# Value-weight loads issued from ScalarE, and a new order of the first value products, in a layernorm, memory-attention and gated-MLP kernel

## The chip, the cores and the metric

The kernel runs on one core of one Trainium2 chip. The metric is the device time of one execution in microseconds (us). The kernel before has a median of 689.46 us in three runs (689.43 to 689.73). Engines are named as the profile names them: PE is TensorE's matmuls, PEld its weight loads, DVE is VectorE, ACT is ScalarE, POOL is GpSimd and SP is SyncE. Loads and stores are DMAs that an engine issues; SPq, ACTq and POOLq are the issuing queues of those engines.

## The reference

One input `x` of 2048 tokens by 448 features goes through a layernorm; attention with a compressed memory over four segments of 512 tokens, and a gated MLP, both read the normalised rows, and their outputs are added to `x`:

```python
x = A_x                                   # 1 x 2048 x 448
xn = _layernorm(x, axis=-1)
return x + _A_ref(xn, A_wq, A_wk, A_wv, A_wo, A_beta) + _B_ref(xn, B_w_gate, B_w_up, B_w_down)
# _A_ref: 16 heads of 28; per segment a causal softmax attention, mixed by sigmoid(beta)
#         with a read of the memory M, z; then M += phi(k)^T v, z += sum phi(k)
# _B_ref: (sigmoid(xn @ w_gate) * (xn @ w_up)) @ w_down
```

What the change touches is the start: the layernorm of the first 512 tokens and `v = xn @ wv` for them.

## The kernel before, in words

The 2048 tokens are four blocks of 512 (`b`), each block four tiles of 128 tokens (`t`). A front part makes values, keys and queries for every block; from then on attention and the MLP are interleaved by a planner. Only the front of block 0 is touched, which is written out by hand: inside it the order of the instructions on PE, ACT and DVE is the order of the code, and the same holds for SP's queue.

Float32 products are made from two rounded parts. A matrix is copied into a rounded type (the high part), and the rest is a subtraction (the low part). A product is then high times high, high times low and low times high. The 448 features are three chunks of 128 and a tail of 64; the tail holds its high part in the upper half and its low part in the lower half of one chunk. So one product of a 128-token tile with the value weights is a list of 11 matmuls of 128 by 448. `EARLY[0]` (L52) lists them in the order that tile 0 and tile 1 use: terms 0 to 2 are high times high, terms 3 to 5 take the low part of the tokens, term 6 is the tail, terms 7 to 9 take the low part of the weights and term 10 the low part of the tail's weights. `value_terms(b, t, pv, terms, n0, n1)` (L333) issues terms n0 to n1.

For one tile the front does this:

- `statistics` (L294 to L296, DVE): mean and variance; `vh` is what the root reads.
- `root` (L301, ACT): a square root, `y`.
- `normalised` calls `rstd` (L308 to L311, DVE) and `normalise` (L320, DVE), which writes `xn`; a strip of 64 columns of it is copied on ACT (L324).
- `turn_high` (L95, PE): four transposes of `xn` into `pt`; then ACT copies the high part into `xs` (L97).
- `turn_low` (L102 and L103, DVE): the low parts of `xs`.
- `split_v(t)` (L431 on ACT, L432 on POOL): high and low part of chunk `t` of the value weights. `raw[0]` and `raw[1]` come from the first load of the weights, `raw[2]` and `raw[3]` from the second.
- `store_values` (L339, ACT): the finished product goes from PSUM to SBUF.

The loads of block 0 are issued by SP one after the other: token tile 0 (L409), tile 1 (L410), the value weights in two halves of 448 KB (L411, L412), token tiles 2 and 3 together (L413), and then the weights of keys and queries (L415 and on) and block 1 (L421). PE starts with 10 matmuls on an identity (`warm`, L442) that compute nothing that is used, and `fill(n)` (L445) issues n more of them; the profile counts two instructions for each.

After the four tiles, `values` for tile 3 and then `keys_queries` (L355, tile `pp`) for block 0 follow on PE.

Of the kernel before, what the change touches and what calls it, by code (L numbers as in the profile page):

```python
# [17 lines left out]
D = 448  # L18
# [33 lines left out]
EARLY = [HIGH + LOW_X + [(3, 3)] + LOW_W + [(3, 7)], HIGH + LOW_W + LOW_X + [(3, 3), (3, 7)]]  # L52
# [9 lines left out]
def kernel(  # L62
# [10 lines left out]
    nc = tc.nc  # L73
# [17 lines left out]
    def transpose_high(pt, src, dst, t):  # L91

        tok = slice(t * P, (t + 1) * P)
        for c in range(4):
            T.transpose(pt[:, c * P:(c + 1) * P], src[:, c * P:(c + 1) * P], ident)  # L95
        p3 = pt.rearrange("p (c n) -> p c n", c=4)
        A.activation(dst[:, 0:4, tok], p3, AF.Copy)  # L97
        return p3

    def transpose_low(p3, dst, t):  # L100
        tok = slice(t * P, (t + 1) * P)
        V.tensor_sub(dst[:, 4:7, tok], p3[:, 0:3], dst[:, 0:3, tok].bitcast(F32))  # L102
        V.tensor_sub(dst[64:, 3, tok], p3[64:, 3], dst[64:, 3, tok].bitcast(F32))  # L103
# [11 lines left out]
    def bank(name, tag):  # L115
        return ps.tile([P, L], F32, name=name, tag=tag, bufs=banks[tag])
# [32 lines left out]
    def four_k(dtype, name):  # L149
        return mid.tile([P, 2, L], dtype, name=name, tag="4k", bufs=4)  # L150
# [125 lines left out]
    with tc.tile_pool(name="front", bufs=2) as sb, tc.manual_schedule(engines=FRONT):  # L276
# [11 lines left out]
        def statistics(b, t0, steps):  # L288

            stats = sb.tile([P, steps, 6], F32, name=f"stats{steps}")  # L290
            mv = sb.tile([P, steps, 2], F32, name=f"mv{steps}")
            vh = sb.tile([P, steps], F32, name=f"vh{steps}")
            for t in range(steps):
                V.bn_stats(stats[:, t, :], acc[b][:, t0 + t, :])  # L294
                V.bn_aggr(mv[:, t, :], stats[:, t, :])
            V.tensor_scalar(vh, mv[:, :, 1], EPS, -0.5, op0=ALU.add, op1=ALU.mult)  # L296
            return mv, vh

        def root(vh):
            y = sb.tile([P, vh.shape[1]], F32, name=f"y{vh.shape[1]}")  # L300
            A.activation(y, vh, AF.Sqrt, scale=-2.0)  # L301
            return y

        def rstd(mv, vh, y):

            steps = vh.shape[1]
            tm = sb.tile([P, steps], F32, name=f"tm{steps}")
            V.reciprocal(y, y)  # L308
            if steps == 1:
                V.tensor_scalar(tm, y, y, vh, op0=ALU.mult, op1=ALU.mult)  # L310
                V.tensor_scalar(y, tm, 1.5, y, op0=ALU.add, op1=ALU.mult)  # L311
            else:
                V.tensor_mul(tm, y, y)
                V.tensor_mul(tm, tm, vh)
                V.scalar_tensor_tensor(y, tm, 1.5, y, op0=ALU.add, op1=ALU.mult)
            return [(mv[:, t, 0:1], y[:, t:t + 1]) for t in range(steps)]

        def normalise(b, t, mean, y):
            xn = sb.tile([P, 512], F32, name="xn")
            V.tensor_scalar(xn[:, :D].rearrange("p (m h c) -> p h m c", h=H, c=4),  # L320
                              acc[b][:, t, :].rearrange("p (h m c) -> p h m c", h=H, c=4), mean, y,
                              op0=ALU.subtract, op1=ALU.mult)
            if b == 0:
                A.activation(xn[:, D:], xn[:, 384:D], AF.Copy)  # L324
            else:
                G.tensor_copy(xn[:, D:], xn[:, 384:D])
            return xn
# [4 lines left out]
        def value_terms(b, t, pv, terms, n0=0, n1=len(TERMS)):  # L332
            for n in range(n0, n1):  # L333
                a, w = terms[n]
                T.matmul(pv[:, :D], xs[b][:, a, t * P:(t + 1) * P], wv[w],  # L335
                         start=n == 0, stop=n == len(TERMS) - 1)

        def store_values(b, t, pv):
            A.activation(vst[:, t, :, :DH], pv[:, :D].rearrange("p (h d) -> p h d", d=DH), AF.Copy)  # L339
            if t == NT - 1:  # L340
                nc.sync.dma_start(vd[b], vst.rearrange("p t h d -> p t (h d)"))
# [65 lines left out]
        raw = [four_k(F32, "wv_raw") for _ in range(2)]  # L407
        raw = [r.rearrange("p a n -> p (a n)")[:, :2 * D] for r in raw]
        nc.sync.dma_start(acc[0][:, 0, :], x[0:P, :])  # L409
        nc.sync.dma_start(acc[0][:, 1, :], x[P:2 * P, :])  # L410
        nc.sync.dma_start(raw[0], w_v[:, :2 * D])  # L411
        nc.sync.dma_start(raw[1], w_v[:, 2 * D:])  # L412
        nc.sync.dma_start(acc[0][:, 2:4, :], x[2 * P:L, :].rearrange("(t p) d -> p t d", p=P))  # L413
        raw = [raw[t // 2][:, t % 2 * D:(t % 2 + 1) * D] for t in range(4)]
        nc.sync.dma_start(stage[:, 0:2, :], w_qk[0:2].rearrange("c p n -> p c n"))  # L415
# [14 lines left out]
        def split_v(t):  # L430
            A.activation(wv[t], raw[t], AF.Copy)  # L431
            G.tensor_sub(wv[4 + t], raw[t], wv[t].bitcast(F32))  # L432
# [10 lines left out]
        def fill(n):  # L443
            for _ in range(n):
                T.matmul(warm[:, :P], ident, ident, start=True, stop=True)  # L445

        def turn_high(t):
            p3[t] = transpose_high(bank("pt", "s"), xn[t], xs[0], t)

        def turn_low(t):  # L450
            transpose_low(p3[t], xs[0], t)

        def normalised(t):
            xn[t] = normalise(0, t, *rstd(*st[t], y[t])[0])

        p3, xn, st, y = {}, {}, {}, {}
        st[0] = statistics(0, 0, 1)
        y[0] = root(st[0][1])
        normalised(0)
        st[1] = statistics(0, 1, 1)  # L460
        y[1] = root(st[1][1])
        turn_high(0)
        fill(5)
        split_v(0)
        split_v(1)
        normalised(1)
        split_v(2)
        split_v(3)
        turn_low(0)
        turn_high(1)  # L470
        st[2] = statistics(0, 2, 1)
        y[2] = root(st[2][1])
        turn_low(1)
        normalised(2)
        st[3] = statistics(0, 3, 1)
        pv = [bank("pv", "p") for _ in range(2)]
        for t in range(2):
            value_terms(0, t, pv[t], EARLY[0], 0, 7)
        value_terms(0, 0, pv[0], EARLY[0], 7)
        store_values(0, 0, pv[0])  # L480
        y[3] = root(st[3][1])
        turn_high(2)
        value_terms(0, 1, pv[1], EARLY[0], 7)
        store_values(0, 1, pv[1])
# [3 lines left out]
        pv = bank("pv", "p")  # L488
# [345 lines left out]
```

## Time and profile before

| | |
|---|---|
| median of three runs | 689.46 us (689.43 to 689.73) |
| the profiled execution's own time | 689.46 us |
| its span, first to last instruction | 687.7 us |
| PE busy in the span | 681.7 us (99%) |
| DVE, ACT and POOL busy | 567.4, 342.6 and 151.3 us |
| mean granted TensorE clock | 0.999 |

The span is 1.76 us shorter than the execution's own time; this rest lies around the instructions. A row of the timeline gives the start in us from the span's start, the duration in us, the engine, the line of the kernel, the operation, what it writes and reads, the shapes, how many instructions are merged in the row, and in brackets how long the engine was idle before and what released it. The line of DMA landings counts from the issue to the arrival.

### The profile page before, as it was taken

Reading aid. Unit: us, or ns where it says so; the run is one execution under the profiler, and the core shown is the slowest. Engines: PE = TensorE matmul, PEld = TensorE weight load, DVE = VectorE, ACT = ScalarE, POOL = GpSimd, SP = SyncE. Lnnn points to the kernel's source line nnn. Section 1 sums busy time; section 2 is a strip of 40 time slices with the busy share of each in tenths; the row PEclk is TensorE's granted clock in tenths of the full one; section 3 lists DMA queues with packets and bytes.
Section 4 is the critical chain, followed back from the end, with each engine's and each line's share of the span. In section 5 each row is a group of like instructions: output and inputs, shape, how many; then the busy total and the mean of one; then the engine's idle time right before and its main releaser. Section 6 shows DMA issues by size and latency. Waiting matters only on the chain.

```text
span 687.7 us, 10438 instructions
## 1 busy us (share of the span) xinstructions
PE 681.7 (99%) x3594; PEld 566.6 (82%) x3594; DVE 567.4 (83%) x994; ACT 342.6 (50%) x563; POOL 151.3 (22%) x349
## 2 busy tenths in 40 slices
PE   8999999999999999999999999999999999999997
PEld 7898888778878787787878878787787878878897
DVE  6765795767788988998898989989898899889863
ACT  4837555343554555543655446454653565446320
POOL 3500020101223222232332222322322322222000
PEclk9999999999999999999999999999999999999999
DMA  7446556696233323243223252314333332423342
GB/s 267 181 150 238 198 214 242 249 330 174 71 94 92 80 86 86 56 128 112 56 64 107 57 141 56 109 47 116 82 94 77 96 71 64 95 79 95 95 153 106
DMA packets 45796, 84.37 MB, mean 123 GB/s; under 512 B 6320, under 2 KB 20400, under 8 KB 45232
## 3 DMA queue, kind: packets, MB, share of 16 engines
q1 hardware_dynamic: 42736, 76.37, 35.8%
q0 software_dynamic: 3008, 7.34, 4.9%
q8 instruction: 28, 0.46, 0.3%
q14 instruction: 24, 0.20, 0.1%
HBM read 51.05 MB, written 32.64 MB: 122 GB/s over the span
## 4 chain that ended last, share of the span: by engine, by line
PE 70%; DVE 14%; issue 9%; POOL 4%; DMA 1%; ACT 1%; SPq 0%; POOLq 0%; ACTq 0%
PE pgu L247 26%; PE pd L173 13%; PE pp L355 10%; PE po L771 5%; PE pv L335 5%; PE st L612 3%; PE pa L687 3%; DVE mx L629 3%; DVE w L666 2%; POOL w L627 2%; DVE acc L174 2%; PE pmm L383 2%; PE n L401 2%; DVE hh L259 1%; DVE mx L633 1%
## 5 line engine op out<-in xcount | busy, mean ns | idle before, releaser
L247 PE MATMUL pgu<-xs,wgu 128*128 128x512 f32 x1232 | 304.1, 394 | 0.0
L247 PEld LDWEIGHTS pgu<-xs,wgu 128*128 128x128 f32 x1232 | 228.2, 188 | 47.4 <-issue 2.2
L173 PE MATMUL pd<-wdn,hh 128*128 128x448 f32 x672 | 156.0, 367 | 0.0
L627 POOL TENSOR_SCALAR_AFFINE_SELECT w<-w 128x256 f32<-128x256 f32 (+1 forms) x160 | 81.2, 509 | 236.4 <-ACT w L616 183.6
L173 PEld LDWEIGHTS pd<-wdn,hh 128*128 128x128 f32 x672 | 122.5, 188 | 12.3 <-issue 0.6
L667 ACT ACTIVATE w<-w 128x1024 f32<-128x1024 f32 (+1 forms) x96 | 87.3, 915 | 65.0 <-DVE w L666 64.2
L666 DVE TENSOR_TENSOR w<-w,mb 128x1024 f32<-128x1024 f32 (+1 forms) x96 | 98.9, 1045 | 0.1
L616 ACT ACTIVATE w<-st 128x512 f32<-128x512 f32 x128 | 74.9, 590 | 45.3 <-PE st L612 44.9
L629 DVE TRANSPOSE_TENSOR_REDUCE mx<-w 128x32 f32<-128x1024 f32 x64 | 79.0, 1235 | 17.0 <-POOL w L627 17.0
L355 PE MATMUL pp<-xs,wqk 128*128 128x512 f32 x308 | 77.7, 401 | 0.0
L174 DVE TENSOR_TENSOR acc<-pd,acc 128x448 f32<-128x448 f32 x112 | 67.1, 599 | 1.2 <-PE pd L173 1.1
L355 PEld LDWEIGHTS pp<-xs,wqk 128*128 128x128 f32 x308 | 56.8, 188 | 13.4 <-issue 2.4
L258 ACT ACTIVATE hh<-sg 128x512 fp32r<-128x512 f32 x56 | 35.2, 628 | 56.4 <-DVE sg L256 49.3
L612 PE MATMUL st<-qk 84*128 84x128 f32 (+3 forms) x256 | 61.9, 312 | 0.0
L255 ACT ACTIVATE sg<-pgu 128x512 f32<-128x512 f32 x56 | 33.2, 594 | 49.4 <-PE pgu L247 49.2
L612 PEld LDWEIGHTS st<-qk 84*128 84x128 f32 x256 | 47.6, 189 | 6.9 <-ACT w L616 0.3
L656 DVE STREAM_TRANSPOSE mb<-top 128x1024 f32<-128x1024 f32 x32 | 39.8, 1242 | 10.5 <-POOL top L653 10.1
L362 DVE TENSOR_TENSOR qk<-pp,qk 128x512 fp32r<-128x512 f32 x28 | 19.3, 688 | 29.8 <-ACT e L360 23.7
L259 DVE SCALAR_TENSOR_TENSOR hh<-sg,hh 128x512 fp32r<-128x512 f32 x56 | 38.7, 691 | 2.6 <-ACT hh L258 2.4
L335 PE MATMUL pv<-wv,xs 128*128 128x448 f32 x176 | 39.6, 376 | 0.4 <-DVE xs L102 0.3
L687 PE MATMUL pa<-w,vv 128*32 128x128 f32 (+3 forms) x512 | 39.7, 436 | 0.2
L256 DVE SCALAR_TENSOR_TENSOR sg<-sg,pgu 128x512 f32<-128x512 f32 x56 | 37.3, 665 | 1.8 <-PE pgu L247 1.6
(100 smaller groups left out, 640.6 us busy)
## 6 DMA issues: line engine op xcount, KB each, us to landing
qk<-qd SPq DMA_DIRECT2D x192, 112.0 KB
qd<-qk SPq DMA_DIRECT2D x28, 512.0 KB
raw<-in_w_ffn SPq DMA_DIRECT2D x14, 512.0 KB
vd<-vst SPq DMA_DIRECT2D x4, 1024.0 KB
vv<-vd SPq DMA_DIRECT2D x16, 256.0 KB
od<-w POOLq DMA_DIRECT2D x16, 256.0 KB, 3.8
sums<-od SPq DMA_DIRECT2D x32, 128.0 KB
out<-acc SPq DMA_DIRECT2D x16, 224.0 KB
```

Of the source, the lines that this page charges most:

```text
L173: T.matmul(pd[:, :D], l, r, start=n == 0, stop=n == len(mms) - 1)
L174: V.tensor_add(acc[b][:, t, :], pd[:, :D], acc[b][:, t, :])
L247: T.matmul(dst, wgu[f][:, w, side * P:(side + 1) * P], xs[b][:, a, :], start=n == 0, stop=n == len(TERMS) - 1)
L335: T.matmul(pv[:, :D], xs[b][:, a, t * P:(t + 1) * P], wv[w], start=n == 0, stop=n == len(TERMS) - 1)
L355: T.matmul(pp, wqk[c][:, w, :], xs[b][:, a, :], start=n == 0, stop=n == len(TERMS) - 1)
L612: T.matmul(st[:, at:at + L - kb * P], self.qk[:KS, 1, h, kb * P:(kb + 1) * P], self.qk[:KS, 0, h, kb * P:], start=True, stop=True)
L616: A.activation(w, st, AF.Copy)
L627: G.affine_select(d, d, pattern=pattern, base=0, channel_multiplier=-1, compare_op=ALU.is_ge, fill=MASK)
L629: V.tensor_reduce(mx[:, 16 * (n - 1):16 * (n + 1)], w3[:, n // 2, :2 * L].rearrange("p (b n) -> p b n", n=32), axis=mybir.AxisListType.X, ...
L666: V.tensor_sub(w, w, m)
L667: A.activation(w, w, AF.Exp, scale=SCALE)
L687: T.matmul(pa[32 * j:32 * j + 32, kb * P:], self.vv[:, kb, 32 * j:32 * j + 32], self.pairs[j // 2].block(j % 2, kb), start=kb == 0, stop=k ...
```

## The change

The two loads of the value weights are issued by ACT's queue instead of SP's, as ACT's first two instructions. The high parts of the weight chunks 0 and 1 (`split_v(0)`, `split_v(1)`) come earlier in ACT's order, one on each side of tile 0's strip copy, ahead of tile 1's root; chunk 2 comes behind tile 0's copy L97, chunk 3 behind tile 1's strip copy. On PE the first three terms of tile 0's product come ahead of tile 1's transposes, 2 fills stand there in place of 5, and the other terms of tiles 0 and 1 are cut in other pieces. Nothing is added to or left out of the computation.

```diff
-        nc.sync.dma_start(raw[0], w_v[:, :2 * D])
-        nc.sync.dma_start(raw[1], w_v[:, 2 * D:])
+        nc.scalar.dma_start(raw[0], w_v[:, :2 * D])
+        nc.scalar.dma_start(raw[1], w_v[:, 2 * D:])
...
         y[0] = root(st[0][1])
+        split_v(0)
         normalised(0)
+        split_v(1)
         st[1] = statistics(0, 1, 1)
         y[1] = root(st[1][1])
         turn_high(0)
-        fill(5)
-        split_v(0)
-        split_v(1)
+        pv = [bank("pv", "p") for _ in range(2)]
+        split_v(2)
+        value_terms(0, 0, pv[0], EARLY[0], 0, 3)
+        fill(2)
         normalised(1)
-        split_v(2)
         split_v(3)
         turn_low(0)
         turn_high(1)
         st[2] = statistics(0, 2, 1)
         y[2] = root(st[2][1])
+        value_terms(0, 0, pv[0], EARLY[0], 3, 10)
         turn_low(1)
         normalised(2)
+        value_terms(0, 1, pv[1], EARLY[0], 0, 3)
+        value_terms(0, 0, pv[0], EARLY[0], 10)
+        store_values(0, 0, pv[0])
         st[3] = statistics(0, 3, 1)
-        pv = [bank("pv", "p") for _ in range(2)]
-        for t in range(2):
-            value_terms(0, t, pv[t], EARLY[0], 0, 7)
-        value_terms(0, 0, pv[0], EARLY[0], 7)
-        store_values(0, 0, pv[0])
         y[3] = root(st[3][1])
+        value_terms(0, 1, pv[1], EARLY[0], 3, 7)
         turn_high(2)
         value_terms(0, 1, pv[1], EARLY[0], 7)
```

SP's order at the program's start, as a difference (L409 and L410 load token tiles 0 and 1, L413 tiles 2 and 3; `acc` holds tokens):

```order
 L409 DMA acc_69<-in_x 128x448
 L410 DMA acc_69<-in_x 128x448
-L411 DMA wv_raw<-in_w_v 128x896
-L412 DMA wv_raw<-in_w_v 128x896
 L413 DMA acc_69<-in_x 128x2x448
 L415 DMA stage<-in_w_qk 128x2x512
```

Two issues have left SP's queue between tile 1 and tiles 2 and 3.

ACT's order at the program's start, before:

```order
L428 ACT_TABLE_LOAD
L428 ACTIVATE gate_n<-vst 128x4
L301 ACTIVATE y_171<-vh_167 128x1
L324 ACTIVATE xn<-xn 128x64
L301 ACTIVATE y_186<-vh_182 128x1
L97 ACTIVATE xs_65<-pt 128x4x128
L431 ACTIVATE wv<-wv_raw 128x448 x2
L324 ACTIVATE xn<-xn 128x64
L431 ACTIVATE wv<-wv_raw 128x448 x2
```

And now (`y_190` is tile 1's root, which was `y_186`):

```order
L411 DMA wv_raw<-in_w_v 128x896
L412 DMA wv_raw<-in_w_v 128x896
L428 ACT_TABLE_LOAD
L428 ACTIVATE gate_n<-vst 128x4
L301 ACTIVATE y_171<-vh_167 128x1
L431 ACTIVATE wv<-wv_raw 128x448
L324 ACTIVATE xn<-xn 128x64
L431 ACTIVATE wv<-wv_raw 128x448
L301 ACTIVATE y_190<-vh_186 128x1
L97 ACTIVATE xs_65<-pt 128x4x128
L431 ACTIVATE wv<-wv_raw 128x448
L324 ACTIVATE xn<-xn 128x64
```

The first split now stands between the root of tile 0 and the strip copy of tile 0, the second between that copy and the root of tile 1.

PE's order at the same place, as a difference (`warm` are the matmuls without use, `pt` the transposes of a tile, `pv` the value products):

```order
 L95 MATMUL pt<-ident,xn 128x128 x4
-L445 MATMUL warm<-ident 128x128 x5
-L95 MATMUL pt<-ident,xn 128x128 x4
-L335 MATMUL pv<-wv,xs_65 128x448 x18
+L335 MATMUL pv<-wv,xs_65 128x448 x3
+L445 MATMUL warm<-ident 128x128 x2
+L95 MATMUL pt<-ident,xn 128x128 x4
+L335 MATMUL pv<-wv,xs_65 128x448 x15
 L95 MATMUL pt<-ident,xn 128x128 x4
 L335 MATMUL pv<-wv,xs_65 128x448 x10
```

Three value matmuls have moved ahead of tile 1's transposes, and three fills are gone; behind tile 2's transposes the order is as it was.

## The prediction

> **What bounds the kernel now.** I read the page's first part, then PE's waits over the whole span, then the chain of waits of the first 30 us, and last the timeline of the same stretch. The page's line of busy times:
>
> ```profile
> PE 681.7 (99%) x3594; PEld 566.6 (82%) x3594; DVE 567.4 (83%) x994; ACT 342.6 (50%) x563; POOL 151.3 (22%) x349
> ```
>
> PE is busy for 99% of the span. Its waits (us in total, times, the longest):
>
> ```profile
> PE warm L442 <- POOL ident masks.py:199: 1.5, 1, 1.5
> PE pt L95 <- DVE xn L320: 0.4, 1, 0.4
> PE pv L335 <- DVE xs L102: 0.3, 1, 0.3
> ```
>
> PE's only waits in 687.7 us are three, all in the first 12 us. So the end moves by what the front moves the point from which PE never stops again. The chain of waits (start, us, what) shows that point:
>
> ```profile
> 1.73 0.42 SPq L411
> ...
> 2.19 0.43 SPq L412
> ...
> 2.67 7.19 DMA acc<-in_x
> ...
> 12.62 0.51 DVE xn L320
> ...
> 14.31 0.49 ACT xs L97
> ...
> 14.85 1.48 PE pv L335 x6
> ...
> 19.99 7.51 PE pp L355 x33
> ```
>
> From 14.85 the chain is PE alone. What sets 14.85 is not PE but the load of token tiles 2 and 3: issued at 2.67 behind the two weight issues, landed at 2.67 + 7.19 = 9.86, then tile 2's statistics on DVE, its `xn` (L320), its copy on ACT (L97). The timeline shows what stands beside it:
>
> ```profile
> 0.81 1.28 ACT L428 ACT_TABLE_LOAD   x1 [0.81 <-PEq L826]
> 1.53 4.64 PE L442 MATMUL warm<-ident 128*128 128x128 f32 x20 [1.53 <-POOL ident masks.py:199]
> 2.10 0.21 ACT L428 ACTIVATE gate_n<-vst 128x4 f32<-128x4 f32 x1
> 3.48 0.63 DVE L294 BATCH_NORM_STATS2 stats<-acc 128x6 f32<-128x448 f32 x1 [3.48 <-DMA acc<-in_x]
> 4.54 0.20 ACT L301 ACTIVATE y<-vh 128x1 f32<-128x1 f32 x1 [2.23 <-DVE vh L296]
> 6.08 0.26 ACT L324 ACTIVATE xn<-xn 128x64 f32<-128x64 f32 x1 [1.34 <-DVE xn L320]
> 6.95 1.28 PE L445 MATMUL warm<-ident 128*128 128x128 f32 x10
> 7.02 0.20 ACT L301 ACTIVATE y<-vh 128x1 f32<-128x1 f32 x1 [0.69 <-DVE vh L296]
> 7.15 0.60 ACT L97 ACTIVATE xs<-pt 128x512 fp32r<-128x512 f32 x1
> 7.59 0.53 SPq L423 DMA_DIRECT2D wqk_raw<-in_w_qk  x1
> 7.64 1.03 ACT L431 ACTIVATE wv<-wv_raw 128x448 fp32r<-128x448 f32 x2
> 8.57 0.25 ACT L324 ACTIVATE xn<-xn 128x64 f32<-128x64 f32 x1
> 9.03 0.29 DVE L103 TENSOR_TENSOR xs<-pt,xs 64x128 fp32r<-64x128 f32 x1
> 9.88 0.63 DVE L294 BATCH_NORM_STATS2 stats<-acc 128x6 f32<-128x448 f32 x1 [0.56 <-DMA acc<-in_x]
> 13.28 0.63 PE L95 MATMUL pt<-ident,xn 128*128 128x128 f32 x4
> 16.52 3.47 PE L335 MATMUL pv<-wv,xs 128*128 128x448 f32 x16
> ```
>
> The reader is to see two DMA waits of DVE: 3.48 us for tile 0, which starts everything, and 0.56 us for tile 2.
>
> **The change part by part.** I call D the time by which tile 0's tokens land later than now (3.48), and write every other time as that of before plus D where it hangs on tile 0.
>
> *SP's queue.* The two issues leave, so the load of tiles 2 and 3 is issued at 1.73 and not at 2.67, 0.94 us earlier. I count this as no earlier landing. The load took 7.19 us from issue to landing, and ahead of it or beside it go the same bytes as before: 224 KB for each of tiles 0 and 1, 896 KB of weights, its own 448 KB. The bound on the good side is 0.53 us: with L103 at 9.03 + 0.29 = 9.32, DVE could take tile 2 at 9.35 and not at 9.88. On the bad side it is nothing, as DVE comes to tile 2 only at 9.35 + D, behind the landing of now once D is over 0.53.
>
> *D itself.* Tile 0's 224 KB went alone ahead of all else. Now 448 KB of weights are issued at the same moment, 0.81, where ACT began its table load. What the transfers moved in each stretch (the last two columns: share of the DMA engines, GB/s):
>
> ```profile
> 1.80:3.50 1.70, 1.70 (x9) 1.70 (x10) 0.02 (x1) 0.50 (x2) 0.50 (x2) 1.00 0.89 275
> 3.50:5.00 1.50, 1.50 (x9) 1.50 (x9) 1.13 (x5) 0.20 (x1) 0.00 (x0) 1.00 0.85 178
> 5.00:7.00 2.00, 2.00 (x11) 1.77 (x11) 1.85 (x6) 0.26 (x1) 0.00 (x0) 1.00 0.96 340
> ```
>
> The DMA engines are at 0.85 or more, so there is no room beside tile 0. If the two loads share evenly, tile 0 waits for nearly all of the 459 thousand bytes: at 340 GB/s 1.35 us, at 275 (tiles 0 and 1) 1.67, at 178 (the weights' first stretch, in which they were slow) 2.58. The lowest end is 0, if tile 0's rows are served first. Two queues side by side are shown once, a 256 KB store of POOL's queue, alone and beside SP's output stores:
>
> ```profile
> od<-w POOLq DMA_DIRECT2D x1, 256.0 KB, 3.8
> ...
> od<-w POOLq DMA_DIRECT2D x1, 256.0 KB, 5.1
> ```
>
> It landed 1.3 us later, so a transfer does pay for its neighbour on another queue. I take D = 1.5, between 1.35 and 1.67 and near 1.3, and keep 0 and 2.58 for the range.
>
> The Trainium skill, page "DMA: Bandwidth & Descriptors", section "Issuing engines are not separate DMA queues", says that loads from several engines run on the same 16 DMA engines and interleave, and that spreading them saves only the issue time. The trace agrees with the first half, with 3.8 against 5.1 us. By that rule the change gains none of the 0.94 us and pays D; without it, with queues of their own, D would be 0 and the sum -0.47.
>
> *ACT's first instructions.* Two issues at SP's rate (0.42, 0.43 and the gaps between: 0.94) push the table load and `gate_n`, which ended at 2.10 + 0.21 = 2.31, to 3.25. The first root starts at 4.54 + D. Cost nothing, cover 1.29 us at least.
>
> *Splits 0 and 1.* The four splits (least, median and most ns of one):
>
> ```profile
> L431 ACT ACTIVATE wv<-wv_raw x4: 562/566/579, 7.6 to 9.2; 128x448 fp32r<-128x448 f32 x4
> ```
>
> One takes 0.57 us. Split 0 stands behind the root (4.74 + D) and ahead of the strip copy (6.08 + D); queued behind it are that copy, then the fourth transpose on PE, then root 1 and so DVE. It costs nothing if the first half of the weights lands by 5.5 + D, at D = 1.5 by 7.0. Now they are in by 7.59, when L423, which SP holds for them, goes out. They are issued 0.92 us earlier, which gives 6.67, so I take nothing. Split 1 goes from 6.34 + D to 6.91 + D, and root 1 at 7.02 + D is just clear of it.
>
> *PE up to tile 2's transposes.* Tile 0's high part is in `xs` at 7.15 + 0.60 = 7.75, plus D. The third term needs split 2, which ACT makes behind L97 at 7.64 + 0.57 = 8.21, so the three terms end at 8.25 + 0.22 = 8.47. Two fills are four instructions at 1.28 / 10 = 0.128 us: 8.98. Tile 1's strip copy, 8.57 + 0.25, is in by then. Four transposes take 0.63: 9.61. Fifteen matmuls at 3.47 / 16 = 0.217 take 3.26: 12.87 + D. Their low parts are there: L103 of tile 0 ended at 9.32, and POOL's splits begin earlier than before.
>
> *DVE up to the same point.* Tile 2's statistics start at 9.35 + D and not 9.88, so its `xn` ends at 13.13 - 0.53 = 12.60 + D, and PE takes tile 2 at 12.87 + D (before 13.28). Its copy L97, behind root 3, is done at 14.31 + 0.49 - 0.53 = 14.27 + D; PE's transposes end at 13.50 and the four last terms of tile 1 at 13.50 + 0.87 = 14.37 + D. So PE begins tile 2's product at 14.37 + D, against 14.84.
>
> **The sum.** The shift is 14.37 + D - 14.84 = D - 0.47, and 1.5 - 0.47 = +1.03 us. Made against the profiled execution's own 689.46 us (span 687.7 and 1.76 around it; the median of the runs is the same 689.46) this is **690.49 us**, 0.15% slower. A measurement of this kernel can tell about 0.2% from no change, 1.38 us; the forecast lies within it, and D decides: from D = 1.85 on the change is slower by more.
>
> **The rivals.**
>
> 1. *Tile 0 waits for the weights at their slow rate* (the other side). The weights' own first stretch ran at 178 GB/s; if tile 0's rows stand behind them one for one, D = 2.58, the shift +2.11, the time 691.57. For it: the 178, and that the slowest of 16 DMA engines sets the landing. Against it: tile 0's own rows flowed in the stretch at 275. It decides from D = 1.85.
>
> 2. *The first split becomes ACT's plug.* If the first weights land no earlier than now, at 7.59, the split ends at 8.16 and the strip copy starts there, not at 6.08: a delay of 2.08 in place of D, a shift of +1.61, 691.07. For it: they share with tile 0. Against it: issued 0.92 us earlier, and tile 1 no longer ahead of them.
>
> 3. *Tile 0 is served first.* D = 0; then the time is between 689.46 (tiles 2 and 3 still land at 9.86) and 688.99 (all 0.47 gained). For it: SP and ACT begin at the same 0.81, so whose rows come first is open. Against it: the 5.1 us. The same skill page, section "Queues, rings and completion order", says that a DMA engine changes between queues only at packet boundaries, a packet being 9 to 17 descriptors as a rule. By that rule tile 0's share of an engine could go out whole ahead of the weights, or whole behind them: D = 0 or rival 1. No row of this trace shows the order of two queues' rows.
>
> 4. *PE's clock falls.* `warm` ran 20 instructions in 4.64 us, 0.232 each, the later fills 0.128: PE sped up by a factor of 1.81 on the way. `warm` ends at 6.17; with D = 1.5 PE then idles to 7.6 and has only transposes until 9.25. If PE fell back, 18 value matmuls at 0.217 would cost 0.81 x 3.9 = 3.2 us more: 693.7. Against it: the longest idle stretch is 1.4 us. The skill's page "TensorE: Matmul & The Clock Gate", section "Part 1: The HAM clock gate", gives about 3.4 us of idleness for a fall, and no run here shows one.
>
> **How the numbers follow.** The forecast, D from 0.5 to 1.85, has a chance of 0.52; rival 1 has 0.24, rival 2 0.09, rival 3 0.12, rival 4 0.03. Slower by over 0.2% are rivals 1, 2 and 4: 0.36. Within 0.2% are the forecast and rival 3, 0.64, of which I take 0.01 off for a gain from a row I have not seen: faster 0.01, same 0.63. The range goes from rival 3's 688.99 to rival 1's 691.57, as 689.0 to 691.6; it leaves out rival 4 and the ends of rivals 1 and 3.
>
> **What would show it.** DVE's first statistics start at 3.48 now; at 4.98 by D = 1.5, at 3.5 by rival 3, at 6 by rival 1. ACT's strip copy of tile 0 should follow `xn` at once; if it follows a split instead, rival 2 holds. The statistics of tile 2 should show no wait for a DMA. The three terms, then two fills, then tile 1's transposes should run without a hole over 0.1 us. Tile 2's product should start near 15.9, and `pp` near 21.0. Forecast and reason are wrong if `pp` starts by 19.99 or over 1.38 us later than that, or if its shift isn't that of the end.

## The result and the profile after

| | before | after |
|---|---|---|
| median of 6 runs each, same chip | 689.47 us (689.42 to 689.73) | 692.76 us (691.87 to 693.25) |
| profiled execution | 689.46 us, span 687.7 | 692.82 us, span 691.1 |
| mean granted TensorE clock | 0.999 | 0.995 |

The ratio is 1.0046, with a 95% interval of 1.0033 to 1.0059: slower by 3.29 us, where 1.03 was forecast and the range ended at 691.6. PE is busy for 682.1 us (99%) as before, so the loss is again to be looked for in the front. The longest of PE's waits in after (us in total, times, the longest):

```profile
PE pt L95 <- DVE xn L320: 2.9, 1, 2.9
```

This wait was 0.4 before. The chain of waits of after:

```profile
0.81 4.27 DMA acc<-in_x
...
7.17 1.15 DVE xn L320
...
8.36 1.13 PE pt L95 x4
...
23.33 6.85 PE pp L355 x30
```

In before this chain ran over the load of tiles 2 and 3 until 14.85. Here it starts with the load of tile 0, and from 8.36 on it is nearly all PE. `pp` starts at 23.33 in place of 19.99: 3.34 us, so all of the loss is there. The timeline of after, the same stretch, shows three things beside one another:

```profile
1.53 3.88 PE L442 MATMUL warm<-ident 128*128 128x128 f32 x20 [1.53 <-POOL ident masks.py:199]
5.11 0.63 DVE L294 BATCH_NORM_STATS2 stats<-acc 128x6 f32<-128x448 f32 x1 [5.11 <-DMA acc<-in_x]
6.93 1.13 POOL L432 TENSOR_TENSOR wv<-wv_raw,wv 128x448 fp32r<-128x448 f32 x1 [4.56 <-ACT wv L431]
7.17 1.14 DVE L320 TENSOR_SCALAR xn<-acc,mv,y 128x448 f32<-128x448 f32 x1
8.36 1.12 PE L95 MATMUL pt<-ident,xn 128*128 128x128 f32 x4 [2.95 <-DVE xn L320]
11.45 1.05 PE L445 MATMUL warm<-ident 128*128 128x128 f32 x4
11.61 0.63 DVE L294 BATCH_NORM_STATS2 stats<-acc 128x6 f32<-128x448 f32 x1
```

- Tile 0's tokens are there at 5.11 (before 3.48): D = 1.63.
- Tile 0's `xn` (L320) takes 1.14 us, where it took 0.51 before (the single row below). It runs beside POOL's first split, 6.93 to 8.06, and ends at 8.31, 0.25 behind it.
- PE runs at half rate: four fills take 1.05, 0.262 each, where those of before took 0.128.

```profile
5.54 0.51 DVE L320 TENSOR_SCALAR xn<-acc,mv,y 128x448 f32<-128x448 f32 x1
```

The third point is the clock. PE's busy time in four stretches of after (start to end, us; PE busy, the count; the third number from the end is the granted clock):

```profile
1.05:4.46 3.41, 2.93 (x13) 2.93 (x14) 0.00 (x0) 1.49 (x2) 1.21 (x5) 1.00 0.69 213
4.46:7.88 3.42, 0.95 (x8) 0.76 (x7) 2.33 (x7) 0.67 (x2) 0.95 (x1) 1.00 1.04 407
7.88:11.29 3.41, 2.24 (x7) 1.76 (x8) 2.93 (x10) 2.46 (x7) 1.94 (x3) 0.50 1.05 385
11.29:14.70 3.41, 3.41 (x14) 3.19 (x14) 1.89 (x6) 0.94 (x3) 1.60 (x2) 0.50 0.97 339
```

The edges are where the trace's clock record changes (4.46 up, 7.88 down, 14.70 up); the steps are one and two times 3.41 us. `warm` filled the first stretch from its start at 1.53 and the clock rose at its end; in the second PE was busy for 0.95 of 3.42 us and the clock fell; for the next 6.82 us it stood at 0.50.

### The profile page after: what moved, and what is told of

Its sections match the earlier page's. It is cut to its first block, busy times and chain, and to the rows that moved or that the text cites. A ratio compares the mean times of both kernels' runs of the same rounds, so it can differ in the third digit from the quotient of the medians.

```text
span 691.1 us, 10426 instructions
## 1 busy us (share of the span) xinstructions
PE 682.1 (99%) x3588; PEld 567.3 (82%) x3588; DVE 568.1 (82%) x994; ACT 342.4 (50%) x563; POOL 151.2 (22%) x349
## 4 chain that ended last, share of the span: by engine, by line
PE 71%; DVE 14%; issue 9%; POOL 4%; ACT 1%; DMA 1%; POOLq 0%; ACTq 0%
PE pgu L247 26%; PE pd L173 13%; PE pp L355 10%; PE pv L335 5%; PE po L773 5%; PE st L614 3%; PE pa L689 3%; DVE mx L631 3%; DVE w L668 2%; POOL w L629 2%; DVE acc L174 2%; PE pmm L383 2%; PE n L401 1%; PE pt L95 1%; DVE hh L259 1%
```

## The experiments

The theory after the result: 3.29 is D − 0.47 = 1.16, plus 0.63 (1.14 − 0.51) by which POOL's split holds `xn` of tile 0, plus about 1.5 by the clock. The rivals: that the new order of products costs the rest by itself; that the two loads on ACT's queue cost all; that the clock alone costs it. Each run below was timed beside the kernel before on the same chip (medians 689.44 to 689.51). The runs of one kernel differ by up to 2.8 us, so ranges are given. The moment at which the first transfers land and the phase of the clock's steps differ from trace to trace and are the likely reasons; there is one trace of each kernel, so this is not shown run by run.

### The loads alone

```diff
 (before)
-        nc.sync.dma_start(raw[0], w_v[:, :2 * D])
-        nc.sync.dma_start(raw[1], w_v[:, 2 * D:])
+        nc.scalar.dma_start(raw[0], w_v[:, :2 * D])
+        nc.scalar.dma_start(raw[1], w_v[:, 2 * D:])
```

> The kernel of before with the two weight loads on ACT's queue, and its old order. Theory A: the 3.3 us of the change are three costs less a gain: tile 0's tokens land 1.63 us later beside the weights, DVE's normalised tile 0 is held 0.63 us by POOL's first split, PE's clock falls to half in the 2.95 us in which PE idles (about 1.6 us), and 0.47 us come back. Here the first and the last remain, as POOL's splits come after the first tile: statistics of tile 0 at 5.1 us, no wait for tiles 2 and 3, 690.5 us if the clock stays and 692 if it falls in PE's gap of some 2 us. Theory B: the new order on ACT and PE is what costs, and the shared loads cost only D - 0.5: 690.5 us with the clock up throughout.

Measured: 691.00 us (690.94 to 691.28, 10 runs), ratio 1.0023 (1.0014 to 1.0032). Its timeline:

```profile
4.96 0.63 DVE L294 BATCH_NORM_STATS2 stats<-acc 128x6 f32<-128x448 f32 x1 [4.96 <-DMA acc<-in_x]
7.02 0.51 DVE L320 TENSOR_SCALAR xn<-acc,mv,y 128x448 f32<-128x448 f32 x1
7.59 0.66 PE L95 MATMUL pt<-ident,xn 128*128 128x128 f32 x4 [1.43 <-DVE xn L320]
9.75 4.61 POOL L432 TENSOR_TENSOR wv<-wv_raw,wv 128x448 fp32r<-128x448 f32 x4 [7.38 <-ACT wv L431]
10.84 0.63 DVE L294 BATCH_NORM_STATS2 stats<-acc 128x6 f32<-128x448 f32 x1
13.58 1.03 DVE L320 TENSOR_SCALAR xn<-acc,mv,y 128x448 f32<-128x448 f32 x1
14.41 0.47 PE L335 MATMUL pv<-wv,xs 128*128 128x448 f32 x1 [0.21 <-POOL wv L432]
```

D is 4.96 − 3.48 = 1.48 and the kernel loses 1.49, all of D. The wait for tiles 2 and 3 is gone (no bracket at 10.84), so by the prediction 0.5 should have come back. It did not: tile 2's `xn` now starts while POOL's splits run (9.75 to 14.36), takes 1.03 and ends at 14.61, again 0.25 behind POOL. PE also waits for POOL directly: the last product before tile 2's transposes reads POOL's last split and starts only at 14.41, when that split has ended (14.36). The two waits end within 0.2 us of one another, so this run cannot tell which of them took the 0.5; both are POOL's splits, which come later by D with tile 0. Tile 0's `xn`, with no split beside it, takes 0.51, and the clock holds through an idle stretch of 1.43. So the loads are 1.5 of the 3.29, and the order has to bring the rest.

### The order alone

```diff
 (after)
-        nc.scalar.dma_start(raw[0], w_v[:, :2 * D])
-        nc.scalar.dma_start(raw[1], w_v[:, 2 * D:])
+        nc.sync.dma_start(raw[0], w_v[:, :2 * D])
+        nc.sync.dma_start(raw[1], w_v[:, 2 * D:])
```

> The changed kernel with the two weight loads back on SP's queue. Theory A: tile 0 lands at 3.48 as before, but split 0 holds ACT until the weights land at 7.6, so tile 0's strip copy starts at 8.2 and not at 6.1; a delay of 2.1, of which 0.5 come back: 691.1 us, and more by up to 1.6 if the clock falls while PE waits for the strip. Theory B (the order costs by itself, in the three terms that wait for their splits): also slower, but with the loss on PE's value matmuls and no late strip. If order and loads are independent of each other, the time is 689.0 to 689.5.

Measured: 690.80 us (689.59 to 692.35, 11 runs), ratio 1.0020 (1.0011 to 1.0029). The profile is of the run with 689.59:

```profile
6.07 0.58 ACT L431 ACTIVATE wv<-wv_raw 128x448 fp32r<-128x448 f32 x1 [1.27 <-DMA wv_raw<-in_w_v]
6.55 0.24 ACT L324 ACTIVATE xn<-xn 128x64 f32<-128x64 f32 x1
```

Split 0 waits 1.27 us for the first weights and holds ACT's queue, the strip copy behind it: rival 2's plug, here without the loads on ACT. In this run it cost only 0.47 (6.55 against 6.08); that later weights cost the slower runs more is likely, but no trace of such a run shows it. POOL's hold is in this run too: tile 1's `xn` takes 1.07, from 8.14 to 9.21, beside POOL's splits. The order alone is slower by 1.29 at the median, and the two halves come to 1.49 + 1.29 = 2.78 of the 3.29.

### The clock

```diff
 (after)
-WARM = 10
+WARM = 18
```

> The changed kernel with 18 matmuls without use at the start in place of 10, so that PE is busy until 7.5 to 8.5 us and not 5.4. Nothing else moves: tile 0 lands at 5.1, its xn is held by POOL. Theory A: the clock stays up, the fills, transposes and value matmuls run at their old durations, 691.2 us (1.6 less than the change). Theory B: the clock is not the cause, 692.8 us or up to 0.3 more.

Measured: 691.28 us (691.13 to 691.49, 8 runs), ratio 1.0027 (1.0016 to 1.0037). Sixteen more instructions without use close the hole, and PE keeps the clock:

```profile
1.53 6.24 PE L442 MATMUL warm<-ident 128*128 128x128 f32 x36 [1.53 <-POOL ident masks.py:199]
8.53 0.66 PE L95 MATMUL pt<-ident,xn 128*128 128x128 f32 x4 [0.76 <-DVE xn L320]
10.96 0.61 PE L445 MATMUL warm<-ident 128*128 128x128 f32 x4
11.76 3.26 PE L335 MATMUL pv<-wv,xs 128*128 128x448 f32 x15
```

The fills are back at 0.15 each and 15 products take 3.26, the time that the prediction used. So the clock costs 692.76 − 691.28 = 1.48; the slowest of these runs is faster than the fastest of after (691.49 and 691.87). `xn` of tile 0 still takes 1.14: the two costs are separate.

### POOL's first split behind `xn`

A one-column copy makes POOL's first subtraction wait for tile 0's `xn`; the subtraction then writes that column anew.

```diff
 (after)
-        split_v(0)
+        A.activation(wv[0], raw[0], AF.Copy)
         normalised(0)
+        G.tensor_copy(wv[4][:, 0:1], xn[0][:, 0:1])
+        G.tensor_sub(wv[4], raw[0], wv[0].bitcast(F32))
         split_v(1)
```

> The changed kernel with POOL's first split made to wait for DVE's xn of tile 0 (a copy of one column of it into the place that the split then overwrites). Theory A: xn takes 0.51 us and not 1.14, tile 0's chain is 0.63 us earlier, 692.1 us; PE's idle time is 2.3 and not 2.95 us, and if that keeps the clock up it is 690.5. If POOL does not hold DVE, xn still takes 1.1 us and the time is 692.8.

Measured: 692.07 us (691.65 to 692.34, 5 runs), ratio 1.0038 (1.0025 to 1.0050). The gain is 0.69 at the median, but the two ranges overlap, and the clock takes another course than in after (below). Its timeline, then PE's busy time between two steps of the clock:

```profile
6.95 0.51 DVE L320 TENSOR_SCALAR xn<-acc,mv,y 128x448 f32<-128x448 f32 x1
7.51 1.12 PE L95 MATMUL pt<-ident,xn 128*128 128x128 f32 x4 [1.36 <-DVE xn L320]
9.43 0.85 DVE L320 TENSOR_SCALAR xn<-acc,mv,y 128x448 f32<-128x448 f32 x1
```

```profile
3.65:7.06 3.41, 2.51 (x12) 2.21 (x11) 1.73 (x7) 0.67 (x2) 0.00 (x0) 1.00 1.03 404
```

`xn` of tile 0 is back at 0.51: POOL's subtraction was what held DVE. (Part of the hold went to tile 1's `xn`, 0.85, as POOL's splits now run later.) And PE's idle stretch is only 1.36, yet the transposes take 1.12, half rate. Here the clock was never raised: the stretch 3.65 to 7.06 was busy for 2.51 of 3.41 us (0.74). The column of the granted clock says 1.00 through all of this, because the trace records only changes of the clock, and here the first change comes at 13.89; the durations show the true rate.

With both repairs together, 18 warming matmuls and the subtraction behind `xn`:

> The changed kernel with both repairs: 18 matmuls without use at the start, and POOL's first split behind xn of tile 0. If the three costs add up as theory A has it, only tile 0's late landing is left, 1.5 to 1.6 less 0.47: 690.5 to 690.6 us. If one of them hid behind another, it is 691.0 or more.

Measured: 690.85 us (690.65 to 691.60, 11 runs), ratio 1.0019 (1.0010 to 1.0028). Against the run with 18 matmuls alone the gain is 0.43, so POOL's hold is worth 0.43 to 0.69 at the medians; the ranges of both pairs overlap, and the hold itself is clearer in the rows (1.14 and 0.51) than in the total times. What is left over before is 1.34 at the median. The trace is of the slowest run, 691.60. In it tile 0 landed at 5.77, so D is 2.29, and tile 1's `xn` took 0.85, 0.34 longer than alone. D − 0.47 + 0.34 = 2.16, against 691.60 − 689.51 = 2.09 lost. So here the 0.47 that the prediction gave back does come back.

### The clock in before

```diff
 (before)
-WARM = 10
+WARM = 3
```

> The kernel of before with 3 matmuls without use at the start in place of 10; all loads as before. It prices the clock alone: PE idles from about 3 to 6.1 us, so the clock comes up one or two windows of 3.4 us later. Theory A: fills, transposes and the first value matmuls run at half speed, 0.8 to 2.5 us slower than before (690.3 to 692), the more the later the clock comes up. If the clock is without weight, 689.5.

Measured: 690.32 us (689.44 to 690.80, 11 runs), ratio 1.0008 (0.9999 to 1.0017); the interval reaches to no change. The profile, of a run with 690.45:

```profile
6.04 1.12 PE L95 MATMUL pt<-ident,xn 128*128 128x128 f32 x4 [2.85 <-DVE xn L320]
6.95 2.34 PE L445 MATMUL warm<-ident 128*128 128x128 f32 x10
```

Ten fills take 2.34 there, and 1.28 before. In before a late clock costs 0.8 at the median and 1.3 at most, and in some runs nothing. A likely reason is that slower matmuls first use up PE's waits for the tiles behind them; no run separates this. Its price is smaller here than in after, and smaller than 0.81 × 3.9 = 3.2, by which rival 4 was priced.

### The loads later

If D comes from two loads that start at one moment, an issue behind `gate_n` should make D zero.

```diff
 (after; the same edit on before with nc.sync)
-        nc.scalar.dma_start(raw[0], w_v[:, :2 * D])
-        nc.scalar.dma_start(raw[1], w_v[:, 2 * D:])
...
         A.activation(gate_n, vst[:, 0, :NG, DH], AF.Sqrt)
+        nc.scalar.dma_start(wv_halves[0], w_v[:, :2 * D])
+        nc.scalar.dma_start(wv_halves[1], w_v[:, 2 * D:])
```

> The changed kernel with ACT's two weight loads behind its table load and its first activation, so issued at about 2.3 and 2.8 us in place of 0.8 and 1.3. Theory A (tile 0's delay comes from weights that flow beside it): tile 0 lands at 3.5 again, PE's idle stretch is gone and with it the fall of the clock, POOL's first split comes behind xn of tile 0; tiles 2 and 3 still land early. All costs are gone and the gain stays: 689.0 us. Theory B (the loads' place on ACT does not matter, the order costs): 690.5 to 692.8.

> The kernel of before, its order unchanged, with the two weight loads on ACT's queue behind its first activation. Tile 0 lands at 3.5, tiles 2 and 3 earlier than 9.86, so DVE's wait for them goes. If POOL's splits hold DVE's xn, as theory A has it, tile 2's xn still ends only when POOL's last split does (12.9 plus 0.25), and the time is that of before, 689.4. If POOL does not hold DVE, 0.5 us come back and it is 689.0.

Measured: 700.77 us (699.98 to 701.11, 4 runs), ratio 1.0160 (1.0146 to 1.0174), and for the order of before 697.65 us (697.47 to 697.88, 4 runs), ratio 1.0116 (1.0101 to 1.0132). Both expectations missed, by 11.8 and 8.3 us, and neither run answers its question. The timeline of the first:

```profile
3.37 0.63 DVE L294 BATCH_NORM_STATS2 stats<-acc 128x6 f32<-128x448 f32 x1 [3.37 <-DMA acc<-in_x]
3.94 0.39 ACTq L428 DMA_DIRECT2D wv_raw<-in_w_v  x1
11.06 0.33 ACTq L429 DMA_DIRECT2D wv_raw<-in_w_v  x1
11.44 0.20 ACT L301 ACTIVATE y<-vh 128x1 f32<-128x1 f32 x1 [9.13 <-DMA wv_raw<-in_w_v]
```

Tile 0 is in at 3.37, but ACT's second issue goes out only at 11.06 (in the other run at 10.69) and the root behind it at 11.44. The issue held ACT's whole queue meanwhile: the root, whose input was ready by 4.4, stood behind it. The chain of waits of this run says what ended the wait: the landing at 11.04 of a load of the key and query weights that SP had issued at 2.71 (10.67 and 2.72 in the other run). ACT's load uses no data of that one. The likely reason is that both report on one semaphore, handed out in the order in which the loads are written. That fits the next runs, where the same loads, written elsewhere, go out at once, but no view shows which semaphore a load uses.

Mended: the memset and `gate_n` are written ahead of all loads, and the two loads stand in their old place, on ACT.

```diff
 (after; the same edit on before with nc.sync there)
+        G.memset(vst[:, :, :, DH:], 1.0)
+        A.activation(gate_n, vst[:, 0, :NG, DH], AF.Sqrt)
         raw = [four_k(F32, "wv_raw") for _ in range(2)]
...
-        G.memset(vst[:, :, :, DH:], 1.0)
-        A.activation(gate_n, vst[:, 0, :NG, DH], AF.Sqrt)
```

> The changed kernel with ACT's table load and first activation written ahead of all loads, so that ACT issues the two weight loads at 2.3 and 2.8 us, and each of the first loads keeps a semaphore of its own (in the two runs before, ACT's second issue waited for an earlier load of SP's to land). Theory A: tile 0 lands at 3.5, PE has no long idle stretch, the clock stays up. What is left is split 0, which holds ACT until the first weights land: at 5.6 us nothing is lost and the time is 689.0; at 6.1, as in the profile of the order alone, it is 689.6; at 7.6 it is 690.8. Theory B (the new order costs by itself): 690.5 or more whatever lands when.

> The kernel of before, its order unchanged, with the weight loads issued by ACT at 2.3 and 2.8 us and semaphores of their own. Tile 0 lands at 3.5, tiles 2 and 3 earlier than 9.86. If POOL's splits hold DVE's xn, tile 2's xn ends only 0.25 us behind POOL's last split (12.9), and the time is that of before, 689.4 to 689.5. If POOL does not hold DVE, 0.5 us come back: 689.0.

Measured: the new order 690.13 us (688.99 to 691.66, 11 runs), ratio 1.0012 (1.0003 to 1.0021); the order of before 689.48 us (689.30 to 689.67, 11 runs), ratio 1.0001 (0.9992 to 1.0009). The new order (a run with 689.29):

```profile
1.30 0.38 ACTq L413 DMA_DIRECT2D wv_raw<-in_w_v  x1
3.47 0.63 DVE L294 BATCH_NORM_STATS2 stats<-acc 128x6 f32<-128x448 f32 x1 [3.47 <-DMA acc<-in_x]
5.36 0.58 ACT L431 ACTIVATE wv<-wv_raw 128x448 fp32r<-128x448 f32 x1 [0.62 <-DMA wv_raw<-in_w_v]
```

The order of before:

```profile
3.39 0.63 DVE L294 BATCH_NORM_STATS2 stats<-acc 128x6 f32<-128x448 f32 x1 [3.39 <-DMA acc<-in_x]
8.17 4.63 POOL L432 TENSOR_TENSOR wv<-wv_raw,wv 128x448 fp32r<-128x448 f32 x4 [5.68 <-ACT wv L431]
9.27 0.63 DVE L294 BATCH_NORM_STATS2 stats<-acc 128x6 f32<-128x448 f32 x1
12.01 1.05 DVE L320 TENSOR_SCALAR xn<-acc,mv,y 128x448 f32<-128x448 f32 x1
12.85 0.47 PE L335 MATMUL pv<-wv,xs 128*128 128x448 f32 x1 [0.23 <-POOL wv L432]
```

The loads go out at 1.30, not at the 2.3 that was expected, and even so an issue 0.49 us later than 0.81 takes D from 1.63 to 0 in both traces. With D gone the new order can reach 688.99, the price that rival 3 had. But split 0 holds ACT until the first weights are in, 0.62 us in this run; times up to 691.66 would fit weights that come later, and no trace of such a run shows it. The order of before gains nothing at all: the 0.5 us of DVE's earlier start (9.27, no wait) is lost to POOL's last split, which ends at 12.80. Tile 2's `xn` is held until then, and so is PE's last product before tile 2's transposes (12.85).

### Moving POOL out of the way

In the order of before with the late issue, POOL's last split behind tile 2's `xn`, and the products that read it behind tile 2's transposes:

```diff
-        split_v(3)
+        A.activation(wv[3], raw[3], AF.Copy)
...
         normalised(2)
+        G.tensor_copy(wv[7][:, 0:1], xn[2][:, 0:1])
+        G.tensor_sub(wv[7], raw[3], wv[3].bitcast(F32))
...
-        value_terms(0, 0, pv[0], EARLY[0], 7)
-        store_values(0, 0, pv[0])
+        value_terms(0, 0, pv[0], EARLY[0], 7, 10)
...
-        value_terms(0, 1, pv[1], EARLY[0], 7)
+        value_terms(0, 1, pv[1], EARLY[0], 7, 10)
+        value_terms(0, 0, pv[0], EARLY[0], 10)
+        store_values(0, 0, pv[0])
+        value_terms(0, 1, pv[1], EARLY[0], 10)
```

> The run before (old order, weights issued by ACT at 1.3 and 1.7 us) with POOL's last split made to wait for DVE's xn of tile 2, by a copy of one column of it; the one term of tile 0 that needs that split, and tile 0's store, come behind tile 2's transposes. If POOL's split is what held xn of tile 2, it now takes 0.51 us and not 1.05, ends at 12.5 and not 13.1, and 0.2 to 0.5 us come through to the end: 689.0 to 689.3 us, below the kernel of before. If something else holds tile 2, the time stays at 689.5.

Measured: 689.77 us (689.65 to 691.37, 11 runs), ratio 1.0008 (0.9999 to 1.0017): a miss, not the gain expected. The timeline:

```profile
12.29 0.51 DVE L320 TENSOR_SCALAR xn<-acc,mv,y 128x448 f32<-128x448 f32 x1
13.14 1.14 POOL L476 TENSOR_TENSOR wv<-wv_raw,wv 128x448 fp32r<-128x448 f32 x1
14.33 0.67 PE L335 MATMUL pv<-wv,xs 128*128 128x448 f32 x2 [0.15 <-POOL wv L476]
15.44 1.49 PE L335 MATMUL pv<-wv,xs 128*128 128x448 f32 x6 [0.43 <-ACT vst L339]
```

`xn` is at 0.51, but the split ends at 14.28 and not at 12.80. PE waits 0.15 for it, and then 0.43 for ACT to empty the accumulators that tile 2 needs. The hold became a wait of PE. So freeing `xn` alone brings nothing, as the product that reads the split waits as well: the split has to go earlier, not later. The last run moves one line of the same base:

```diff
         normalised(0)
+        split_v(0)
         st[1] = statistics(0, 1, 1)
...
         fill(5)
-        split_v(0)
         split_v(1)
```

> The order of before with the loads on ScalarE's queue behind `gate_n` (as in the run with 689.48), and the first split alone moved ahead, between tile 0's strip copy and tile 1's root; the other three splits follow tile 0's copy L97 and tile 1's strip copy. Nothing is left out.
>
> By POOL holding VectorE: POOL's first split goes out at about 6.9 and no longer at 8.17, its last ends near 11.7 and no longer at 12.80, so tile 2's `xn`, which starts at 12.01, takes 0.51 us and not 1.05. PE has its own work until 12.62 + 0.22 = 12.84 and takes tile 2's transposes there, not at 13.20: 0.36 us earlier, 689.1 us. The condition is that the first weights have landed by 6.3; a run in which they land later delays tile 1's root, and each us behind that costs one, up to 690.7.
>
> By the rival, that `xn` of tile 2 is not what the end hangs on, as in the run that put POOL's last split behind it: 689.4 to 689.5 with `xn` at 0.51.
>
> By the other rival, that POOL meets tile 1's `xn` instead, at 7.93, and delays it by 0.1 or more: the gain is that much less, 689.2 to 689.3.

Measured: 689.11 us (688.98 to 690.07, 11 runs), ratio 0.9996 (0.9987 to 1.0005). The profile is of a run with 689.73, in which tile 0 landed only at 4.12, so the late issue does not make D zero in every run (0.64 here):

```profile
9.70 3.38 POOL L432 TENSOR_TENSOR wv<-wv_raw,wv 128x448 fp32r<-128x448 f32 x3
12.74 0.58 DVE L320 TENSOR_SCALAR xn<-acc,mv,y 128x448 f32<-128x448 f32 x1
```

Tile 2's `xn` takes 0.58 and no longer 1.05; it ends 0.24 behind POOL even so. PE no longer waits for POOL: its 18 products run through. The median is the 689.1 that was expected, 0.38 us below before, but the interval takes in 1, so a gain over the kernel before is not shown.

## Why the prediction was wrong, point by point

- *SP's queue.* Right in what it counted: tile 2's statistics no longer wait (11.61), and no gain came from the earlier issue by itself. That the load lands no earlier was too cautious where it can be seen: in the order of before with the late loads, tile 2 was in by 9.27, and before at 9.86.
- *D.* Right in size: 1.5 taken, 1.63 measured. The other traces with both loads issued at 0.81 have 1.48, 1.80, 1.41 and 2.29, so the closeness is in part luck. Whether the rows of the two loads really alternate, as the even share has it, no run shows. The slow rate of the weights that made rival 1 did not come back: 178 GB/s in their first stretch before, and now in after:

```profile
3.50:5.00 1.50, 1.50 (x11) 1.50 (x11) 0.00 (x0) 0.00 (x0) 0.00 (x0) 1.00 1.04 412
```

- *Splits 0 and 1.* This is the step of the sum that failed: "I take nothing". (The larger part of the miss, 1.48, is rival 4, which stood outside the sum.) The weights were in time, as it said: split 0 runs at 6.29 without a wait. It asked when ACT would run split 0 and what stood behind it on ACT. It did not ask what POOL would do the moment split 0's copy was ready: start a subtraction of 1.13 us beside the `xn` that everything waits for. Price: 0.63 in the trace, 0.43 to 0.69 by the runs. The trace of before had the sign of it, in rows that the prediction did not use:

```profile
29.96 1.27 POOL L437 TENSOR_TENSOR wqk<-wqk_raw,wqk 128x512 fp32r<-128x512 f32 x1
30.66 0.83 DVE L320 TENSOR_SCALAR xn<-acc,mv,y 128x448 f32<-128x448 f32 x1
```

  The Trainium skill, page "SBUF — State Buffer", section "Who interferes with whom", says that VectorE in its two-port modes and GpSimd share one pair of ports as an exclusive lock, that whoever issues first has it for the whole instruction while the other blocks, and that `tensor_scalar` is one of the operations that can take it. The runs agree: 1.14 beside POOL, 0.51 as soon as POOL's subtraction was moved. No view shows the mode in which DVE ran.
- *Rival 4, the clock.* The mechanism was named and given 0.03, against it "the longest idle stretch is 1.4 us". That stretch was taken from `warm` ending at 6.17 and `xn` ending 0.5 after its start. In after `warm` ended at 5.41, since the clock rose earlier, and `xn` late: 2.95 us. But the run with the subtraction behind `xn` shows that even 1.36 us was too much at another phase of the steps. What decided, by these traces, was how busy PE was between two steps: 2.51 of 3.41 us in that run, where before had PE at work through the whole of the stretch:

```profile
3.46:6.87 3.41, 3.41 (x17) 3.18 (x17) 2.88 (x10) 0.46 (x2) 0.00 (x0) 1.00 0.90 265
```

  Its size was wrong as well: 1.48, not 3.2. And PE did not speed up within `warm` in before, as "sped up by a factor of 1.81 on the way" can be read: 20 instructions at 0.232 are the slow rate throughout, as 2.93 us for the first 13 show in after, and the fills behind it were the first at the fast rate.
- *DVE up to tile 2.* The term of −0.47 was worked out right for PE and DVE as the prediction had them, but in the run with the loads alone nothing of it came (1.49 lost at a D of 1.48): POOL's last split came later by D too, and both `xn` and a product of PE waited for it. With the new order and both repairs it came, as far as one trace shows (2.09 lost at a D of 2.29).
- *The sum.* 1.16 + 0.63 + 1.48 = 3.27 against 3.29 measured. That it fits so closely is in part luck, as two terms are from one trace and the third is from medians; repaired one after the other, the runs give 1.48 for the clock, 0.43 for POOL's hold and 1.34 that is left. Of the sum the forecast had the first term, 1.03. Of the signs it named, the landing (5.11 for 4.98), the strip copy right behind `xn` and tile 2 without a wait came true; `pp` at 23.33 for 21.0 did not.

## What to carry to other kernels

Moving an operation earlier moves the second half of it earlier too, on another engine: ask what that engine will run beside the operation that everything waits for, and whether the two hold one another; rows of the same operation with unlike durations in the trace of before are where this shows. If a start gets later by a us or two, count how busy TensorE is in each stretch of 3.4 us until the work is steady, and not only the longest hole. Of two loads, the one that gates the start should be issued ahead of the bulk, not together with it: 0.49 us took away the whole delay in three of four traces here, and most of it in the fourth.

## What the runs showed of the hardware

- DVE's `xn` beside a POOL subtraction ended 0.25 us behind POOL in after (8.31 and 8.06), 0.25 with the loads alone (14.61 and 14.36), 0.26 in the order of before with the late loads (13.06 and 12.80), 0.24 in the last run (13.32 and 13.08), however long ago it had begun. DVE's statistics beside POOL kept their 0.63 (10.84, with the loads alone).
- The clock changed only at steps of 3.41 us. It was raised behind stretches in which PE was busy for 0.86 of the time (1.05 to 4.46 in after, 2.93 of 3.41) and 0.80 (the first row below, of the run with the loads alone), not behind 0.66 (7.88 to 11.29 in after) and 0.74 (the run with the subtraction behind `xn`); it fell behind 0.28 (4.46 to 7.88 in after), and held behind 0.57 (the second row):

```profile
3.44:6.85 3.41, 2.72 (x13) 2.42 (x12) 1.48 (x6) 0.20 (x1) 0.00 (x0) 1.00 1.03 401
6.85:10.26 3.41, 1.96 (x16) 1.77 (x17) 2.93 (x10) 2.00 (x7) 0.51 (x1) 1.00 1.05 392
```

  The Trainium skill, page "TensorE: Matmul & The Clock Gate", section "Part 1: The HAM clock gate", gives free-running windows of 3413 ns and a fall after an idle window; the steps agree, and a window that was 28% busy counted as idle here.
- 0.49 us between two issues decided over 1.5 us of landing time of the first: tile 0 landed at 5.11 with the loads issued together, and at 3.47, 3.39, 3.48 and once at 4.12 with the weights 0.49 us later.
- An issue of ACT's that had to wait held ACT for 6.7 us (4.33 to 11.06, the run with 700.77), with no instruction of ACT's to show for it.
